# Attention with a gated MLP on one core: per-block output priority, a reciprocal as exp(-ln) on ScalarE, and a new order of the last four blocks

## The chip, the cores and the metric

The kernel runs on one core of a Trainium2 chip. A core has five engines that each work through a queue of their own in order: TensorE (PE, matrix products, with PEld for its weight loads), VectorE (DVE), ScalarE (ACT, activation functions), GpSimd (POOL) and SyncE (SP, which issues DMAs). Engines wait for each other through semaphores. The metric is device time in microseconds of one execution; lower is better.

## The reference

One token stream `x` of 2048 rows and 448 columns is normalised, and goes through attention with 16 heads of 28 columns and through a two-layer MLP; the product of the two branches is added to `x`:

```python
xn = _layernorm(x, axis=-1)
# A: attention
qkv = (xn @ wqkv).reshape(B, S, 3, H, Dh)      # H = 16, Dh = 28
scores = jnp.einsum("bhqd,bhkd->bhqk", q, k) * Dh ** -0.5
p = _softmax(scores, axis=-1)
o = jnp.einsum("bhqk,bhkd->bhqd", p, v)
s = o.reshape(B, S, D) @ wo
# B: MLP
h = _gelu(jnp.einsum("bsd,df->bsf", xn, w1) + b1)   # F = 1792
g = _silu(jnp.einsum("bsf,fd->bsd", h, w2) + b2)
return x + s * g
```

All arrays are bfloat16.

## The kernel before

**Blocks.** The attention is cut into 16 blocks (`NBLK`): four groups `g` of four heads, times four chunks `c` of 512 query rows. Block 4g+c has 64 steps `m`, each the scores of 128 keys against 512 queries for one head. Three more stages run beside the blocks: projections early, the MLP's first layer and GELU in the middle, its second layer (`p_f2`, 16 tiles), the gate (`p_silu`) and the output product with `wo` (`p_out`, `p_last`, 16 tiles of 128 rows) at the end. The output product of chunk c needs all four groups, so block 12+c (group 3) must be finished and normalised first.

**Softmax.** Scores of two or three steps go into banks of a PSUM ring (`t_score`), ScalarE takes exp of the two or three banks with one instruction (`p_exps`, 1024 or 1536 columns wide), and `t_pv` multiplies the result with the values and adds up in the bank `acc`. One column of the values gives the row sums. Some steps do not go through ScalarE: four steps at a time (a "quad") are sent to VectorE, which makes an approximate exp with integer arithmetic (`p_apass`, four instructions of 512 columns, then two more in `p_expq`); such steps are left out of ScalarE's list. `NQ` says how many quads each block tries for.

**Normalising a block.** `p_epi` copies `acc` to `E_sb` on VectorE, sends the four rows of sums by DMA to DRAM (`sums`) and back spread over 128 partitions (`rs`), takes the reciprocal on GpSimd (`rc`, a power of -1), sends it to DRAM (`recs`) and back broadcast (`x_sb<-recs`, four DMAs), and multiplies on GpSimd into `qT`. The last block is handled by quarters of 128 queries `t`: `p_epi4` copies a quarter out of `acc` (the last one on ScalarE, `EA = 1`), `p_norm4` spreads the sums over the partitions with one matmul against `selb`, takes a reciprocal on VectorE and multiplies; `p_last` then makes the output tile.

**Output tiles.** `t_oev` multiplies a finished `wo` product with the gate, adds `x` for chunks 2 and 3, and stores. A tile that comes after the last exp is copied from PSUM by ScalarE first, for those listed in `PATH`. The gate of the very last tile is made at the end (a tanh on ScalarE, two VectorE instructions).

**What sets the order.** A planner inside the kernel (`run`) lays down all five queues before anything executes. It keeps estimated durations for every task, and picks the next task of an engine by start time, then by a priority number (small goes first). Per block, `tune` overwrites a set of planner constants from the table `BP`: how early quads start, how many go with a group of scores, how many ring banks a group may take (`R3`), when the `t_pv` products are due, and so on. Which banks, fillers and quads fall where follows from these constants alone.

Of the kernel before, what the change touches and what calls it, by code (L numbers as in the profile page):

```python
# [16 lines left out]
DH = 28  # L17
F = 1792
G = 4
# [8 lines left out]
MTOT = NBLK * T * 4  # L28

GM = 584  # L30
BPN = ('MG', 'GQ', 'GE', 'EPS', 'PV0', 'PVC', 'MP', 'ND4', 'LU', 'JOINT', 'LQ', 'JMAX', 'DQ', 'URG', 'SLACK', 'UR', 'QLEAD', 'QDIST', 'R3')
BP = (
    (0, 7.789, 12, 0.114, 12, 2, 0.127, 4, 18, 0.15, 2, 2, 1, 7, 0.379, 1.063, -8, 20, 2),
    (0, 4.0, 12, 0.103, 12, 3, 0.124, 4, 16, 0.116, 2, 4, 8, 8, 0.359, 0.922, 18, 20, 0),
    (0, 4.0, 12, 0.1, 12, 3, 0.124, 4, 16, 0.02, 2, 3, 8, 9, 0.285, 0.922, 60, 31, 1),
    (1, 4.0, 11, 0.151, 12, 3, 0.124, 3, 14, 0.034, 2, 4, 10, 2, 0.413, 0.922, 58, 45, 1),
    (1, 4.0, 12, 0.1, 10, 4, 2.634, 4, 16, 0.232, 3, 5, 12, 17, 0.678, 0.922, -8, 20, 1),
    (1, 4.0, 12, 0.133, 18, 4, 0.124, 4, 17, 0.15, 2, 2, 8, 3, 0.413, 0.922, 60, 26, 1),
    (0, 4.0, 10, 0.143, 20, 1, 0.124, 6, 0, 0.15, 3, 5, 10, 4, 0.476, 2.281, 62, 36, 0),
    (0, 4.0, 22, 0.1, 29, 3, 0.034, 4, 15, 0.227, 6, 4, 6, 14, 0.306, 0.922, 60, 2, 3),  # L40
    (1, 4.0, 29, 0.182, 11, 1, 1.508, 2, 18, 0.237, 2, 4, 8, 8, 0.413, 0.922, 62, 12, 1),
    (1, 2.818, 8, 0.1, 6, 3, 0.124, 6, 5, 0.099, 5, 4, 8, 14, 0.378, 5.756, 60, 22, 1),
    (0, 4.0, 9, 0.079, 13, 3, 0.124, 5, 14, 0.094, 2, 2, 2, 22, 0.234, 0.623, 11, 12, 0),
    (0, 4.619, 12, 0.1, 12, 3, 0.124, 8, 2, 0.15, 2, 4, 6, 8, 0.244, 0.922, 60, 24, 0),
    (0, 5.612, 13, 0.1, 9, 2, 0.124, 4, 18, 0.375, 2, 4, 8, 9, 0.413, 0.922, -2, 16, 1),
    (1, 3.195, 12, 0.129, 17, 3, 0.124, 1, 0, 0.249, 2, 4, 10, 12, 0.413, 1.834, 60, 20, 1),
    (1, 4.0, 12, 0.109, 12, 3, 0.188, 4, 16, 0.131, 2, 4, 9, 22, 0.413, 0.922, 60, 20, 0),
    (0, 4.0, 12, 0.1, 12, 9, 0.124, 6, 18, 0.132, 2, 3, 8, 5, 0.342, 1.07, 56, 20, 2),
    (1, 4.0, 12, 0.1, 12, 3, 0.124, 4, 16, 0.15, 2, 4, 8, 10, 0.413, 0.922, 60, 20, 1),
)  # L50
NQ = (5, 11, 13, 13, 12, 7, 11, 10, 16, 3, 16, 16, 9, 14, 16, 16)
QLEAD, QDIST = 0, 12
JMAX, DQ, LQ, ND4, LU = 2, 3, 2, 3, 3
PV0, PVC, MP = 12, 4, 0.3
# [6 lines left out]
GP, MP4, GL = 4.64, 1, 1.2  # L61
URG = 12
SPR, AHEAD = 5, 101
R3 = 0
DUE, UR, M0, M2 = 13, 1.25, 59, 978
VT = (15, 14, 13, 12, 11, 10, 9, 8)
SM_SCALE = DH ** -0.5
# [21 lines left out]
EPS = 0.1  # L89
PVN = 2  # L90
OWN2 = 0
EA = 1
G3P = 0
PATH = {(1, 2): 'D', (1, 3): 'D', (2, 0): 'D', (2, 1): 'D', (2, 2): 'D', (2, 3): 'D'}
XADD = ()
OPR = (5, 5, 5)
OVERLAP = 0.083


# [26 lines left out]
class _Kernel:  # L126
# [258 lines left out]
    def alloc(self):  # L385
# [126 lines left out]
        self.b_selb = B()  # L512
        self.b_E4, self.b_on4, self.b_o4, self.b_o3 = ([B() for _ in range(4)] for _ in range(4))
        self.b_rf = [B(), B()]
        self.b_sum, self.b_sum2, self.b_m3 = B(), B(), B()
        self.b_sig3, self.b_g3 = B(), B()
        self.banks = [(self.misc[:, :], self.b_misc), (self.acc[:, :], self.b_acc)]
# [837 lines left out]
    def p_silu(self, c):  # L1355
        K = self
        yield ("until", lambda: K.f2n[c] == 4 and K.ready([K.b_fsb[c % 2]], 0.3) and (c < 2 or K.g_done[c - 2]))
        fb, sg = K.fsb[:, c % 2, :, :], K.sig[:, c % 2, :, :]
        nt = 4 if c < C - 1 else 3
        yield _Task(ACT, lambda eng: eng.activation(sg[:, 0:nt, :], fb[:, 0:nt, :], ACTF.Tanh, scale=0.5),  # L1360
                    [K.b_fsb[c % 2]], [K.b_sig[c % 2]], 0.1 + 0.375 * nt, 0.0, 0)
        if c < C - 1:
            for t in range(nt):
                o = K.g_sb[:, c, t, :]
                yield _Task(POOL, lambda eng, o=o, t=t: eng.tensor_tensor(o, sg[:, t, :], fb[:, t, :], ALU.mult),  # L1365
                            [K.b_sig[c % 2], K.b_fsb[c % 2]], [K.b_h[c], K.b_g[c]], 1.05, 0.05, 3, port=True)
                yield _Task(POOL, lambda eng, o=o, t=t: eng.tensor_tensor(o, o, fb[:, t, :], ALU.add),
                            [K.b_sig[c % 2], K.b_fsb[c % 2]], [K.b_h[c], K.b_g[c]], 1.05, 0.05, 3, port=True)
        for t0 in range(0, nt if c == C - 1 else 0, 2):
            t1 = min(t0 + 2, nt)  # L1370
            yield _Task(DVE, lambda eng, t0=t0, t1=t1: eng.scalar_tensor_tensor(
                K.g_sb[:, c, t0:t1, :], sg[:, t0:t1, :], 1.0, fb[:, t0:t1, :], op0=ALU.add, op1=ALU.mult),
                        [K.b_sig[c % 2], K.b_fsb[c % 2]], [K.b_h[c], K.b_g[c]], 0.15 + 0.467 * (t1 - t0), 0.0, 3)
        K.g_done[c] = True
        if c == C - 2:
            K.b_x2[c].r = list(K.b_h[c].r) + [K.b_h[c].w]
            for y in K.b_h[1], K.b_h[2]:
                K.b_x2[c].r += y.r + [y.w]
            xc = K.A_x[0].rearrange("(c p t) d -> c p t d", p=128, t=4)[c]
            for i in range(OWN2 // 2, 2):  # L1380
                dst = K.h[:, 1 + i, 5632:5632 + 2 * D].rearrange("p (t d) -> p t d", d=D)
                K.dma(SP, lambda eng, i=i, dst=dst: eng.dma_start(dst, xc[:, 2 * i:2 * i + 2, :]), K.s_x3, writes=[K.b_x2[c]] if i else [])
        if c < C - 1:
            return
        K.b_x2[c].r = list(K.b_h[c].r) + [K.b_h[c].w]
        K.dma(SP, lambda eng: eng.dma_start(K.x2[1][:, :, :], K.A_x[0].rearrange("(c p t) d -> c p t d", p=128, t=4)[c]),
              K.s_x2[c], writes=[K.b_x2[c]])
        if nt < 4:
            yield ("until", lambda: K.exp_m == MTOT - 1)
            o = K.g_sb[:, c, 3, :]  # L1390
            yield _Task(ACT, lambda eng: eng.activation(sg[:, 3, :], fb[:, 3, :], ACTF.Tanh, scale=0.5),
                        [K.b_fsb[c % 2]], [K.b_sig3], 0.47, 0.0, 0)
            E = POOL if G3P else DVE
            if not G3P:
                yield ("until", lambda: K.E_done == NBLK + 1)
            yield _Task(E, lambda eng: eng.tensor_tensor(o, sg[:, 3, :], fb[:, 3, :], ALU.mult),
                        [K.b_sig3, K.b_fsb[c % 2]], [K.b_h[c], K.b_g3], 1.05 if G3P else 0.39, 0.0, 2, port=E == POOL)
            if not G3P:
                yield ("until", lambda: K.on4[3])
            yield _Task(E, lambda eng: eng.tensor_tensor(o, o, fb[:, 3, :], ALU.add),  # L1400
                        [K.b_fsb[c % 2]], [K.b_h[c], K.b_g3], 1.05 if G3P else 0.39, 0.0, 2, port=E == POOL)

    def pieces(self, m):
        b, r = m // 64, m % 64
# [494 lines left out]
    def p_norm4(self, t):  # L1899
        K = self  # L1900
        g, c = G - 1, C - 1
        E, tE = K.E_sb[:, 1, 128 * t:128 * (t + 1)], K.b_E4[t]
        bank, tok = yield ("bank", lambda: K.g_done[C - 1] and K.ready([tE]), 3)
        yield _Task(PE, lambda eng: eng.matmul(bank[:, 0:128], K.selb[:, :], E, start=True, stop=True),
                    [tE, K.b_selb], [tok], 0.1, 0.12, 3)
        R = K.rf[:, t % 2, :]
        yield _Task(DVE, lambda eng: eng.reciprocal(R, bank[:, 0:128]), [tok], [K.b_rf[t % 2]], 0.96, 0.0, 1)
        K.banks.append((bank, tok))
        dst = K.qT[:, g, c * 512 + 128 * t:c * 512 + 128 * (t + 1)]
        yield _Task(DVE, lambda eng: eng.tensor_tensor(dst, E, R, ALU.mult), [tE, K.b_rf[t % 2], K.b_qT[g][c]],  # L1910
                    [K.b_on4[t]], 0.3, 0.0, 1)
        K.on4[t] = True

    def p_epi(self, b):
# [7 lines left out]
        yield ("until", lambda: K.late_on)  # L1922
        lag = 2.2 if b >= NBLK - 4 else 4.0
        src = bass.AP(tensor=K.E_sb, offset=DH * 1024 + 512 * (b % 2), ap=[[32 * 1024, 4], [1, 512]])
        K.dma(SP, lambda eng: eng.dma_start(K.sums.ap(), src), K.s_r[0], reads=[tE], writes=[K.b_sums],
              land=max(K.now, tE.tw) + lag)
        K.dma(SP, lambda eng: eng.dma_start(K.rs[:, :], K.sums.ap().rearrange("j (i k) -> (j i) k", k=16)), K.s_r[1],
              reads=[K.b_sums], writes=[K.b_srs], land=K.b_sums.tw + lag)
        yield _Task(POOL, lambda eng: eng.tensor_tensor(K.rc[:, :], K.rs[:, :], K.mone[:, 0:1].to_broadcast([128, 16]), ALU.pow),  # L1929
                    [K.b_srs, K.b_pads], [K.b_rc], 3.0, 0.05, 1)  # L1930
        K.dma(SP, lambda eng: eng.dma_start(K.recs.ap().rearrange("j (i k) -> (j i) k", k=16), K.rc[:, :]), K.s_r[2],
# [46 lines left out]
    
    def p_out(self, c, t):
        K = self  # L1980
        bank, tok = yield ("bank", lambda: K.pe_free() and K.on_done[(G - 1) * C + c] and K.g_done[c] and K.ready(K.b_onT[G - 1][c:c + 1]), OPR[c])
        K.pe_wait += 1
        ps = bank[:, 0:D]
        yield K.t_wo(ps, tok, c, t, (0, 1))
        yield K.t_wo(ps, tok, c, t, (2, 3))
        K.pe_wait -= 1
        yield from K.t_oev(ps, tok, c, t)
        K.banks.append((bank, tok))
# [63 lines left out]
```

## Time and profile before

| what | us |
|---|---|
| median of 3 runs (421.92 to 422.02) | 422.02 |
| the profiled execution's own time | 422.14 |
| its span, first to last instruction | 420.4 |
| TensorE busy | 401.6 |
| ScalarE busy | 406.6 |
| VectorE busy | 338.9 |
| GpSimd busy | 186.0 |
| granted TensorE clock, mean | 0.998 |
| window 302.47 to 341.60: ScalarE busy, VectorE busy | 38.75, 32.68 of 39.13 |
| window 341.60 to 391.60: ScalarE busy, VectorE busy | 49.98, 39.04 of 50.00 |
| window 391.60 to 410.34: ScalarE busy, VectorE busy | 18.74, 15.36 of 18.74 |
| window 410.34 to 420.40: ScalarE busy, TensorE busy | 3.02, 4.27 of 10.06 |

The four windows lie between the starts of the `acc` copies of blocks 10, 12 and 14, the end of the last exp, and the end of the span. Busy times are unions of an engine's instructions; activations overlap at their ends, so the sum of their durations is more than the time that they take, and the distance between two starts is the better measure. The engines' names and the source lines (L1480 is line 1480 of the kernel) are those of the profile.

### The profile page before, as it was taken

The numbers are of one execution on the slowest core, as the hardware profiler recorded it, in microseconds if no ns is written. First come the engines' busy times: TensorE is split into PE (matmuls) and PEld (weight loads), VectorE is DVE, ScalarE is ACT, GpSimd is POOL, SyncE is SP. The second block draws the span as 40 slices with busy tenths as digits, with TensorE's granted clock in tenths as the row PEclk, the third lists the DMA queues.
The fourth block names the chain that finished last, engine by engine and source line by source line (L and its number), as shares of the span: only waits on it lengthen the run. The fifth ranks groups of instructions, "written<-read, shape, count | busy, mean of one in ns | idle before, by whom it ended". The sixth has DMA issues, their size and how long they took to land.

```text
span 420.4 us, 9639 instructions
## 1 busy us (share of the span) xinstructions
PE 401.6 (96%) x3673; PEld 135.2 (32%) x3673; DVE 338.9 (81%) x588; ACT 406.6 (97%) x413; POOL 186.0 (44%) x193
## 2 busy tenths in 40 slices
PE   6999999999999999999999999999999999999994
PEld 4543223332222222223223433232222333223452
DVE  8968899997785899999893126799999675599885
ACT  6999999999999999999999999999999999999993
POOL 7571333237769271213331514408221947882420
PEclk9999999999999999999999999999999999999999
DMA  8701000000001001010320100000010001014142
GB/s 264 268 2 39 3 7 22 20 11 16 25 2 27 2 1 29 2 27 16 86 85 26 27 1 2 2 2 27 2 26 3 10 21 27 2 47 93 24 72 90
DMA packets 15912, 15.29 MB, mean 36 GB/s; under 512 B 7085, under 2 KB 12953, under 8 KB 15834
## 3 DMA queue, kind: packets, MB, share of 16 engines
q1 hardware_dynamic: 15002, 13.07, 11.1%
q0 software_dynamic: 576, 0.92, 1.7%
q8 instruction: 29, 0.48, 0.5%
q10 hardware_dynamic: 288, 0.69, 0.4%
q14 instruction: 17, 0.14, 0.1%
HBM read 12.60 MB, written 2.94 MB: 37 GB/s over the span
## 4 chain that ended last, share of the span: by engine, by line
PE 69%; ACT 15%; DVE 8%; issue 6%; POOL 1%; DVEq 0%; ACTq 0%; POOLq 0%
PE ring L1424 21%; PE acc L1860 16%; ACT P L1480 9%; PE ring L1275 9%; PE ring L1344 5%; PE ring L920 3%; ACT h L1480 3%; PE misc L920 3%; PE misc L1344 2%; ACT xnT L1480 2%; PE misc L1275 2%; PE misc L1214 2%; PE misc L1948 1%; PE ring L1214 1%; PE acc L1061 1%
## 5 line engine op out<-in xcount | busy, mean ns | idle before, releaser
L1480 ACT ACTIVATE P<-ring 128x1024 bf16<-128x1024 f32 (+1 forms) x238 | 253.5, 1179 | 1.4 <-PE ring L1424 0.6
L1424 PE MATMUL ring<-qT,kT 32*128 32x512 bf16 (+2 forms) x1049 | 141.9, 357 | 8.2 <-ACT P L1480 1.3
L1480 ACT ACTIVATE h<-ring 128x1024 bf16<-128x1024 f32 (+1 forms) x80 | 87.2, 1190 | 0.1
L1424 PEld LDWEIGHTS ring<-qT,kT 32*128 32x128 bf16 x1049 | 38.6, 91 | 143.4 <-ACT P L1480 82.9
L1929 POOL TENSOR_TENSOR rc<-rs,mone 128x16 f32<-128x16 bf16 x15 | 45.5, 3032 | 36.6 <-DMA rs<-sums 36.5
L1860 PE MATMUL acc<-P,vaug 128*32 128x512 bf16 (+2 forms) x621 | 53.9, 351 | 0.0
L1275 PE MATMUL ring<-xnT,w 128*128 128x512 bf16 x180 | 48.9, 382 | 0.0
L1480 ACT ACTIVATE xnT<-ring 128x1024 bf16<-128x1024 f32 (+1 forms) x37 | 43.1, 1203 | 0.1
L1938 POOL TENSOR_TENSOR qT<-x_sb,E_sb 128x512 bf16<-128x512 f32 x15 | 17.4, 1162 | 48.4 <-PE acc L1860 15.5
L1424 PE MATMUL misc<-qT,kT 32*128 32x512 bf16 (+1 forms) x103 | 38.4, 378 | 0.0
L1344 PE MATMUL ring<-w,h 128*128 128x448 bf16 x154 | 37.4, 355 | 0.4 <-DVE vaug L1709 0.3
L1709 DVE TENSOR_SCALAR x_sb<-ring 128x512 uint16<-128x512 f32 x40 | 27.1, 686 | 1.9 <-PE ring L1424 1.3
L1169 POOL TENSOR_TENSOR qsq<-qT 128x512 bf16<-128x512 bf16 x12 | 12.5, 1039 | 33.9 <-DVE qT L1163 31.4
L1860 PE MATMUL acc<-h,vaug 128*32 128x512 bf16 x222 | 27.1, 384 | 0.0
L1709 DVE TENSOR_SCALAR x_sb<-misc 128x512 uint16<-128x512 f32 x28 | 19.2, 686 | 4.8 <-PE misc L1424 4.0
L1275 PEld LDWEIGHTS ring<-xnT,w 128*128 128x128 bf16 x180 | 14.7, 97 | 23.8 <-issue 8.3
L1365 POOL TENSOR_TENSOR h<-w 128x448 bf16<-128x448 bf16 x12 | 12.7, 1055 | 21.8 <-DVE h L1768 14.5
L1709 DVE TENSOR_SCALAR h<-ring 128x512 uint16<-128x512 f32 x28 | 19.0, 686 | 0.3 <-PE ring L1424 0.2
L1860 PEld LDWEIGHTS acc<-P,vaug 128*32 128x32 bf16 x621 | 13.5, 95 | 16.3 <-issue 12.4
L1793 POOL TENSOR_SCALAR vs<-vaug 128x128 bf16<-128x128 bf16 x32 | 9.5, 297 | 20.6 <-DVE w L1768 18.0
L1259 DVE CAST h<-ring 128x512 bf16<-128x512 f32 x21 | 14.4, 686 | 4.4 <-PE ring L1275 4.3
L1344 PE MATMUL misc<-w,h 128*128 128x448 bf16 x70 | 17.1, 355 | 0.0
(266 smaller groups left out, 695.4 us busy)
## 6 DMA issues: line engine op xcount, KB each, us to landing
x_sb<-recs SPq DMA_DIRECT2D x60, 64.0 KB, 2.0
w<-in_B_w_dram SPq DMA_DIRECT2D x1, 1568.0 KB, 7.3
w<-in_B_w_dram SPq DMA_DIRECT2D x1, 1344.0 KB, 8.2
x_sb<-in_A_x_dram SPq DMA_DIRECT2D x2, 448.0 KB, 5.4
out_dram<-in_A_x_dram SPq DMA_DIRECT2D x2, 448.0 KB, 9.3
out_dram<-h POOLq DMA_DIRECT2D x4, 224.0 KB, 4.3
out_dram<-h SPq DMA_DIRECT2D x8, 112.0 KB, 1.7
h<-in_A_wqkv_dram SPq DMA_DIRECT2D x3, 168.0 KB, 5.1
```

The source lines that it names most:

```text
L920: return eng.matmul(bank, w[:, k, g * 128:(g + 1) * 128], K.xnT[:, k, c * 512:(c + 1) * 512], start=(k == 0), stop=(k == KT - 1))
L1214: ins = eng.matmul(bank[:, off:off + nh * DH], K.xnT[:, kt, t * 128:(t + 1) * 128], ap, start=(kt == 0), stop=(kt == KT - 1), skip_group_c ...
L1259: yield _Task(DVE, lambda eng: eng.tensor_copy(dst, bank), [tok], wr, 0.69, 0.0, 2)
L1275: return eng.matmul(bank, K.w1[:, k, ft * 128:(ft + 1) * 128], K.xnT[:, k, c * 512:(c + 1) * 512], start=(k == 0), stop=(k == KT - 1))
L1344: ins = eng.matmul(ps, hv[:, ft, t * 128:(t + 1) * 128], K.w2[:, ft, :], start=(ft == 0), stop=(ft == FT - 1))
L1365: yield _Task(POOL, lambda eng, o=o, t=t: eng.tensor_tensor(o, sg[:, t, :], fb[:, t, :], ALU.mult), [K.b_sig[c % 2], K.b_fsb[c % 2]], [K.b ...
L1424: return eng.matmul(dst, K.kT[32 * j:32 * j + 32, g, t * 128:(t + 1) * 128], K.qT[32 * j:32 * j + 32, g, c * 512 + q0:c * 512 + q0 + nq], ...
L1480: return eng.activation(reg[:, i0:i0 + n, :], K.ring[:, b0:b0 + n, :], ACTF.Exp, scale=SM_SCALE)
L1709: yield _Task(DVE, lambda eng: eng.tensor_scalar(K.part(u, k).bitcast(dt.uint16), K.like(u, bank), SM_SCALE * LOG2E * 128.0, (127.0 - EXP_ ...
L1860: return eng.matmul(K.acc[32 * j:32 * j + 32, q0:q0 + nq], w, ap[:, col:col + nq] if len(ap.shape) == 2 else ap[:, col // 128:(col + nq) / ...
L1929: yield _Task(POOL, lambda eng: eng.tensor_tensor(K.rc[:, :], K.rs[:, :], K.mone[:, 0:1].to_broadcast([128, 16]), ALU.pow), [K.b_srs, K.b_ ...
L1938: yield _Task(POOL, lambda eng: eng.tensor_tensor(dst, K.rb, E, ALU.mult), [K.b_rb, tE], [K.b_onT[g][c]], 1.15, 0.05, 1, port=True)
```

## The change

The diff has four parts.

1. A 20th column `OP` in the table: the priority of the output tiles of chunks 0 to 2, which was 5 for each, is 5 in blocks 0 to 12, then 4.26 in block 13, 5.041 in block 14 and 2.148 in block 15.
2. Rows 12 to 15 of the table have new numbers, and blocks 14 and 15 try for 14 quads where it was 16.
3. In the last block the last quarter's copy out of `acc` goes from ScalarE to VectorE (`EA = 0`); its reciprocal is made on ScalarE by ln and exp with a table load ahead of it (`LNR = 1`); and the spreading matmul may take a PSUM bank 0.35 us (planned) before its input is there.
4. Block 14's sums go straight from `E_sb` to `rs` in four small DMAs, where there was one to DRAM and one back.

```diff
-    (0, 5.612, 13, 0.1, 9, 2, 0.124, 4, 18, 0.375, 2, 4, 8, 9, 0.413, 0.922, -2, 16, 1),
-    (1, 3.195, 12, 0.129, 17, 3, 0.124, 1, 0, 0.249, 2, 4, 10, 12, 0.413, 1.834, 60, 20, 1),
-    (1, 4.0, 12, 0.109, 12, 3, 0.188, 4, 16, 0.131, 2, 4, 9, 22, 0.413, 0.922, 60, 20, 0),
-    (0, 4.0, 12, 0.1, 12, 9, 0.124, 6, 18, 0.132, 2, 3, 8, 5, 0.342, 1.07, 56, 20, 2),
+    (0, 5.612, 13, 0.1, 10, 4, 0.124, 4, 18, 0.375, 5, 4, 6, 9, 0.413, 0.922, 0, 12, 0, 5.0),
+    (1, 3.195, 12, 0.129, 6, 6, 0.124, 1, 0, 0.042, 1, 4, 10, 12, 0.413, 1.834, 77, 20, 1, 4.26),
+    (1, 5.574, 19, 0.109, 12, 5, 0.266, 3, 16, 0.061, 3, 3, 8, 4, 0.606, 0.922, 52, 39, 1, 5.041),
+    (0, 6.398, 12, 0.169, 12, 9, 0.124, 6, 18, 0.132, 2, 3, 8, 5, 0.342, 1.07, 56, 20, 2, 2.148),
...
-NQ = (5, 11, 13, 13, 12, 7, 11, 10, 16, 3, 16, 16, 9, 14, 16, 16)
+NQ = (5, 11, 13, 13, 12, 7, 11, 10, 16, 3, 16, 16, 9, 14, 14, 14)
...
-EA = 1
+EA = 0
+LNR = 1
...
+            if LNR:
+                K.prog[ACT].append(lambda eng: eng.preload_act_table_set("natural_log_exp_and_others"))
+                K.tE[ACT] += 1.3
...
-        bank, tok = yield ("bank", lambda: K.g_done[C - 1] and K.ready([tE]), 3)
+        bank, tok = yield ("bank", lambda: K.g_done[C - 1] and K.ready([tE], 0.35), 3)
...
-        yield _Task(DVE, lambda eng: eng.reciprocal(R, bank[:, 0:128]), [tok], [K.b_rf[t % 2]], 0.96, 0.0, 1)
+        if LNR and t == 3:
+            yield _Task(ACT, lambda eng: eng.activation(R, bank[:, 0:128], ACTF.Ln), [tok], [K.b_rf[t % 2]], 0.25, 0.0, 0)
+            yield _Task(ACT, lambda eng: eng.activation(R, R, ACTF.Exp, scale=-1.0), [K.b_rf[t % 2]], [K.b_rf[t % 2]], 0.25, 0.05, 0)
+        else:
+            yield _Task(DVE, lambda eng: eng.reciprocal(R, bank[:, 0:128]), [tok], [K.b_rf[t % 2]], 0.96, 0.0, 1)
...
+        if b == NBLK - 2:
+            for j in range(4):
+                one = bass.AP(tensor=K.E_sb, offset=(32 * j + DH) * 1024 + 512 * (b % 2), ap=[[1024, 1], [16, 32], [1, 16]])
+                K.dma(SP, lambda eng, j=j, one=one: eng.dma_start(K.rs[32 * j:32 * j + 32, :], one), K.s_r[1],
+                      reads=[tE], writes=[K.b_srs] if j == 3 else [], land=max(K.now, tE.tw) + lag)
...
-        bank, tok = yield ("bank", lambda: K.pe_free() and K.on_done[(G - 1) * C + c] and K.g_done[c] and K.ready(K.b_onT[G - 1][c:c + 1]), OPR[c])
+        bank, tok = yield ("bank", lambda: K.pe_free() and K.on_done[(G - 1) * C + c] and K.g_done[c] and K.ready(K.b_onT[G - 1][c:c + 1]), lambda: OP)
```

What this makes of the queues can be read from the built programs, without any time in them. All five queues are the same up to block 12. From there on:

| | before | changed |
|---|---|---|
| exps on ScalarE of 1024, 1536, 512 columns, from block 12's first group on | 51, 31, 1 | 55, 30, 0 |
| quads on VectorE, whole kernel | 59 | 58 |
| VectorE instructions between the `acc` copies of blocks 10 and 12 | 52 | 62 |
| output tiles behind the last exp on VectorE | 5, and the addition of a sixth | 3 |
| ScalarE copies of output tiles | 4 | 0 |
| exps between block 14's `acc` copy and chunk 2's first `wo` product | all that are left | about 9, each of 1536 |

Behind the last exp the changed queues hold, on TensorE: the last 32 `acc` products, one `wo` product, the spreading matmul, and two tiles of four `wo` products each; on ScalarE: the tanh of the last gate, the table load, ln, exp; on VectorE: the `acc` copy, a tile (multiply, add), half of the last gate, the last quarter's multiply, a tile, the other half of the gate, the last tile.

## The prediction

> **What bounds the kernel now.** I read the page first: busy shares and slices.
>
> ```profile
> PE 401.6 (96%) x3673; PEld 135.2 (32%) x3673; DVE 338.9 (81%) x588; ACT 406.6 (97%) x413; POOL 186.0 (44%) x193
> ACT   6999999999999999999999999999999999999993
> PE 69%; ACT 15%; DVE 8%; issue 6%; POOL 1%; DVEq 0%; ACTq 0%; POOLq 0%
> ```
>
> The third line is the chain of waits in the page's section 4; it names TensorE for most of the span, but a busy TensorE is not one that is late: ScalarE is full in every slice but the first and the last. So I took ScalarE's timeline (start, us, what; a row is a run of equal instructions).
>
> ```profile
> 302.09 7.46 ACT L1480 ACTIVATE P<-ring 128x1024 bf16<-128x1024 f32 x8
> 309.37 1.11 ACT L1480 ACTIVATE xnT<-ring 128x1024 bf16<-128x1024 f32 x1
> 389.83 2.87 ACT L1480 ACTIVATE xnT<-ring 128x1536 bf16<-128x1536 f32 x2
> 392.49 8.33 ACT L1480 ACTIVATE P<-ring 128x1536 bf16<-128x1536 f32 x7
> 405.04 5.40 ACT L1480 ACTIVATE P<-ring 128x1536 bf16<-128x1536 f32 x5
> 410.34 0.57 ACT L1391 ACTIVATE w<-w 128x448 bf16<-128x448 bf16 x1
> 411.28 0.28 ACT L1889 ACTIVATE E_sb<-acc 128x128 bf16<-128x128 f32 x1 [0.38 <-PE acc L1860]
> 412.13 0.54 ACT L1961 ACTIVATE h<-ring 128x448 bf16<-128x448 f32 x1 [0.57 <-PE ring L1948]
> ```
>
> Starts are what counts, since ends overlap. Eight exps of 1024 run from 302.09 to 309.37 with one short wait among them; the bare step is 0.904. Two of 1536 take 392.49 - 389.83 = 2.66, 1.33 each. The last exp is over at 410.34 (the tanh of L1391 follows at once), and 420.4 - 410.34 = 10.06 us of tail are left. The time is thus: ScalarE's work up to the last exp, plus its waits, plus the tail.
>
> **Part 1, ScalarE's work: +1.8.** The queues part at 315.77, where block 12's first exp starts. Before: 51 x 0.904 + 31 x 1.33 + 0.49 (the one of 512) + three tanhs (1.60, 1.60, 1.23, by their starts) = 92.25. Changed: 55 x 0.904 + 30 x 1.33 + 4.43 = 94.05. One quad less on VectorE is four steps more here. This is a count; I give it 0.1 either way. It is on the path.
>
> **Part 2, ScalarE's waits: -0.3.** Before, 410.34 - 315.77 = 94.57, so 94.57 - 92.25 = 2.32 us were waits, in pieces of 0.04 to 0.4. To see what the new order does to them I walked down two queues, TensorE's and ScalarE's, with distances between starts from TensorE's timeline: a score group 0.32 until other work starts, four `acc` products 0.215, two second-layer products 0.378, two `wo` products 0.38, 0.10 for going back to scores; a group starts 0.06 after the exp two before it ended and its exp at the earliest 0.45 later. For the queues before, this gives 1.4 of the 2.3, most of it where six or seven second-layer products stand between two groups (324.6 in the trace is one such place: `misc<-w,h` x10). In the new order fillers are spread more evenly and the walk gives 0.2. What the walk doesn't see (0.9 before: VectorE's banks, tanhs that wait for their input) I carry over at 0.8. From 0.5 to 1.5 for both together.
>
> A new wait comes on top. Chunk 2's first `wo` product now stands in TensorE's queue about nine exps of 1536, 9 x 1.33 = 12.0, behind the `acc` copy of block 14, with score groups queued behind it, and ScalarE waits for those. The chain that it needs, as it ran before:
>
> ```profile
> 391.60 0.69 DVE L1919 CAST E_sb<-acc 128x512 bf16<-128x512 f32 x1 [0.59 <-PE acc L1860]
> 392.32 0.49 SPq L1925 DMA_DIRECT2D sums<-E_sb  x1
> 393.93 0.34 SPq L1927 DMA_DIRECT2D rs<-sums  x1
> 395.59 3.44 POOL L1929 TENSOR_TENSOR rc<-rs,mone 128x16 f32<-128x16 bf16 x1 [5.65 <-DMA rs<-sums]
> 399.05 0.32 SPq L1931 DMA_DIRECT2D recs<-rc  x1
> 400.46 2.54 SPq L1934 DMA_DIRECT2D x_sb<-recs  x4
> 405.48 1.14 POOL L1938 TENSOR_TENSOR qT<-x_sb,E_sb 128x512 bf16<-128x512 f32 x1 [4.43 <-PE acc L1860]
> ```
>
> That is 15.02 us from copy to product. The direct DMAs take out one trip (393.93 - 392.32 = 1.61) but put four issues on SP in place of one: at steps of about 0.43 (the sixteen small `wo` loads at 33 us) the last leaves 1.3 after the first, and lands 1.6 after that (the row's median for `rs`), so `rc` starts 3.6 after the copy where it was 4.0: 0.4 gained, not 1.6. The rest varied over the 15 blocks: `rc` 2.9 to 3.44, the broadcast 3.3 to 4.9 from first issue to landing. So the chain takes 12.4 to 14.6. TensorE can wait until 12.4 after the copy before ScalarE runs dry (one exp of 0.904 and 0.45 of score time ahead, 0.96 for the four products in between). That is 0 to 2.3 us; block 14's broadcast was the slow one, beside GpSimd's output DMA, which stands in the same place now. I take 1.0. Waits in all: 0.2 + 0.8 + 1.0 = 2.0, against 2.32.
>
> **Part 3, the tail: -2.7.** Before, VectorE ended it:
>
> ```profile
> 411.11 0.39 DVE L1396 TENSOR_TENSOR h<-w 128x448 bf16<-128x448 bf16 x1
> 412.57 0.96 DVE L1907 RECIPROCAL w<-misc 128x128 f32<-128x128 f32 x1 [1.07 <-PE misc L1904]
> 416.53 0.69 DVE L1969 TENSOR_TENSOR h<-h 128x448 bf16<-128x448 bf16 x2
> L1327 ACT ACT_TABLE_LOAD x1 | 1.3, 1283 | 0.0
> ```
>
> The spreading matmul stood behind six `wo` products, the reciprocal idled 1.07 for it, and 12 instructions of chunks 2 and 3 followed until 417.21 (6.88 after the last exp); the last store was issued at 417.64. Changed, counted from the last exp: `acc` products done 0.89 (as before), copy 0.94 to 1.23, spreading matmul 1.46 to 1.68 behind one `wo` product. ScalarE: tanh to 0.57, table load 1.283 with 0.02 around it (it followed an exp 0.02 after its end at 252.46, and the next exp 0.01 after it), so ln starts at 1.87, after the matmul; ln and exp at about 0.3 each (the 128-column copy took 0.28) end at 2.5. VectorE meanwhile adds one tile and the gate's half (1.3 to 2.47), multiplies the quarter at 2.57, then tile (0.53 + 0.30), gate half 0.30, last tile 0.53 + 0.39: 4.85. Store at 4.9 against 7.30: 2.4 less. The last store landed 2.23 after issue, the others 1.7; with 0.3 for that, 2.7. From 2.0 to 3.1. The copy goes from ScalarE (0.28) to VectorE, idle then, at no cost. The table load is hidden by copy and matmul but for 1.87 - 1.73 = 0.14; without that cover it costs its 1.3.
>
> For the table switch, the Trainium skill (ScalarE: Activation LUTs, section "What ACT_TABLE_LOAD costs") states about 1283 ns for the load plus about 1380 ns of drain, 2.66 us for every switch. Ln would then start at 3.2 and the tail gain 1.3 instead of 2.7. The load's duration agrees to the nanosecond; the drain does not show in this trace, where load and its gaps take 1.31.
>
> Block priorities (`OP`) cost nothing by themselves: they moved chunk 2's four tiles ahead of the last exp, into TensorE's slack under the exps; without that cover they cost what the tail now saves.
>
> **Sum.** +1.8 - 0.3 - 2.7 = -1.2 on the profiled execution's 422.14 (420.4 of span, 1.7 around it), 420.9. The median of the runs is 0.1 lower: 420.8.
>
> **Rivals.**
> *No wait at chunk 2* (chain 12.4): waits 1.0, sum -2.2, 419.8. For it: the broadcast took 3.3 in most blocks. Against: not in block 14.
> *Full wait* (chain 14.6), or other waits as large as before: waits 3.3, sum +0.1, 422.1. For it: the planner's order fits a chain of 12, and GpSimd's DMAs stand beside it.
> *The table switch drains first*, for as long as the load itself takes (1.283, the row above): ln, exp and the five VectorE instructions behind them come 1.28 later, sum +0.1, 422.1. Against it: both loads inside the span followed their exp after 0.02. (The Trainium skill's section named above states such a drain.)
> *VectorE becomes the bound in blocks 11 and 12* (the other side). Between the copies of blocks 10 and 12 it now has 62 instructions for 40.3 us of ScalarE work, where it had 52 for 37.4 (32.68 busy of 39.13). For it, its rhythm in this stretch before:
>
> ```profile
> 317.99 0.69 DVE L1709 TENSOR_SCALAR wq<-misc 128x512 uint16<-128x512 f32 x1
> 318.60 0.68 DVE L1768 TENSOR_SCALAR vaug<-x_sb 128x2048 uint16<-128x2048 uint16 x1
> 319.26 0.69 DVE L1709 TENSOR_SCALAR wq<-misc 128x512 uint16<-128x512 f32 x1
> ```
>
> Two instructions take 319.26 - 317.99 = 1.27, so 62 need 39.4, just under 40.3. At 0.69 each, without overlap, they need 42.8 and ScalarE loses 2.5: sum +1.3, 423.3. It decides from 0.65 per instruction on; beside GpSimd's multiply at 405.48 one VectorE instruction (L1910) took 1.07 instead of 0.28, so stretching occurs. Against it: between 156 and 182 us VectorE was busy for 25.75 of 26, and ScalarE still for 25.99.
> *The change doesn't do what it says* has little room: the queues show each part.
>
> **How the numbers follow.** Forecast 0.45, no wait 0.15, full wait 0.18, drain 0.05, VectorE 0.17. About 0.2%, 0.84 us, is what a measurement of this kernel can tell from no change: faster is under 421.2, slower over 422.9. The first two are faster (0.60); full wait and drain are the same (0.23); VectorE is slower (0.17). The forecast's own range is 420.2 to 421.2 (chunk 2's wait between 0.4 and 1.4). The range goes from 419.4 (waits of 1.0 and a tail of -3.1) to 423.2 and so leaves out little more than half of the last case.
>
> **What would show it.** Last exp about 1.5 us later than 410.3 (411.8), tail of 7.4; TensorE idle before chunk 2's first `wo` product (L1962) with GpSimd's L1952 as releaser, about 1.0 in ScalarE's waits behind it; `rc` (L1943) of block 14 starting 3.6 after its copy; ln starting within 0.2 of the table load's end; ScalarE idle for VectorE's banks in block 12 under 0.8. A tail over 8.5, or waits over 3.5 in the last four blocks, would make it wrong.

## The result and the profile after

| | before | changed |
|---|---|---|
| median, us | 422.02 (5 runs, 421.9 to 422.13) | 427.41 (5 runs) |
| ratio, 95% interval | | 1.0126 [1.0112, 1.014] |
| span of the profiled execution | 420.4 | 425.5 |
| its granted clock, mean | 0.998 | 0.989 |

The changed kernel is 1.3% slower. Four of its runs lie between 426.44 and 428.72; one took 1173.25, which nothing here explains; the ratio leaves it out, and nothing below rests on it.

The page of the changed kernel first: busy shares, two of the slices, the chain of waits, and the group of exps (busy, mean ns of one, then idle time before it and who ended that).

```profile
PE 403.9 (95%) x3667; PEld 133.4 (31%) x3667; DVE 336.1 (79%) x582; ACT 407.8 (96%) x413; POOL 189.6 (45%) x197
ACT  6999999999999999999999999999999999999935
PEclk9999999999999999999999999999999999999968
PE 73%; ACT 12%; DVE 8%; issue 5%; DMA 1%; POOLq 0%; ACTq 0%; DVEq 0%
L1484 ACT ACTIVATE P<-ring 128x1024 bf16<-128x1024 f32 (+1 forms) x241 | 256.3, 1179 | 7.7 <-PE ring L1428 6.8
```

The fourth line is the chain of waits: it now has a share for DMA, 1% or some 4 us, which it had not before. ScalarE is full until the last two slices, where before only the last was thin; now the last but one is down to the digit 3 as well, and the clock falls to 0.6 there. The idle time that the exps spend on score groups, 6.8 us, is nearly all new: it was 0.6 before. ScalarE's timeline of the last 25 us shows where it lies (start, us, what; idle time before it and its releaser in brackets):

```profile
400.34 2.99 ACT L1484 ACTIVATE xnT<-ring 128x1536 bf16<-128x1536 f32 x2
403.00 1.25 ACT L1484 ACTIVATE P<-ring 128x1024 bf16<-128x1024 f32 x1
408.82 2.42 ACT L1484 ACTIVATE P<-ring 128x1536 bf16<-128x1536 f32 x2 [4.57 <-PE ring L1428]
413.12 5.05 ACT L1484 ACTIVATE P<-ring 128x1536 bf16<-128x1536 f32 x4 [1.88 <-PE ring L1428]
418.03 0.60 ACT L1392 ACTIVATE w<-w 128x448 bf16<-128x448 bf16 x1
418.64 1.28 ACT L1395 ACT_TABLE_LOAD   x1
419.94 0.28 ACT L1912 ACTIVATE w<-ring 128x128 f32<-128x128 f32 x1
```

Two waits, 4.57 and 1.88 as the trace counts them. Measured between starts, as the prediction did, they are 408.82 - 403.00 - 0.90 = 4.92, and 413.12 - 410.21 - 0.90 = 2.0 (the row at 408.82 names its first form only: its second exp, at 410.21, is one of 1024). The last exp ends at 418.03, not at 411.8; the tail behind it is 425.5 - 418.03 = 7.47.

So the 5.1 us of the spans divide into ScalarE's work +1.8, its waits from 2.32 to 8.29 (+5.97), and the tail from 10.06 to 7.47 (-2.6); the sum is +5.2, 0.1 over what the spans show.

What the waits hang on is block 14's way from `acc` to its multiply, and what lies around it:

```profile
389.86 0.68 DVE L1927 CAST E_sb<-acc 128x512 bf16<-128x512 f32 x1
390.56 2.50 SPq L1936 DMA_DIRECT2D rs<-E_sb  x4
392.02 0.87 POOL L1988 DMA_DIRECT2D out_dram<-h  x1 [3.12 <-DVE h L1979]
396.24 2.92 POOL L1943 TENSOR_TENSOR rc<-rs,mone 128x16 f32<-128x16 bf16 x1 [3.35 <-DMA rs<-E_sb]
399.13 0.90 POOL L1988 DMA_DIRECT2D out_dram<-h  x1
400.62 1.75 SPq L1948 DMA_DIRECT2D x_sb<-recs  x4
401.23 0.86 POOL L1988 DMA_DIRECT2D out_dram<-h  x1 [1.19 <-PE ring L1428]
406.10 1.15 POOL L1952 TENSOR_TENSOR qT<-x_sb,E_sb 128x512 bf16<-128x512 f32 x1 [4.02 <-DMA x_sb<-recs]
407.31 0.93 PE L1962 MATMUL ring<-wo,qT 128*128 128x448 bf16 x2 [4.16 <-POOL qT L1952]
408.17 0.61 PE L1428 MATMUL ring<-qT,kT 32*128 32x128 bf16 x12
```

The power (`rc`) starts 6.38 after the copy, where before's two trips gave 3.98, and the multiply 16.24 after it. TensorE stands for 4.16 before chunk 2's first product, with the score group for ScalarE behind it in its queue. The windows (length, busy time of PE, PEld, DVE, ACT and POOL, granted clock, share of the DMA engines, GB/s) show what follows:

```profile
403.00:408.80 5.80, 1.64 (x16) 0.58 (x16) 1.58 (x3) 1.25 (x2) 1.15 (x1) 0.78 0.38 69
408.80:412.00 3.20, 3.20 (x16) 1.11 (x16) 1.38 (x4) 2.42 (x2) 0.00 (x0) 0.50 0.11 36
412.00:418.00 6.00, 5.46 (x121) 2.88 (x120) 3.85 (x9) 4.88 (x4) 0.00 (x0) 0.91 0.18 60
```

Behind the pause the granted clock is 0.50. A score group takes 0.61 (the row at 408.17) instead of 0.40, and now TensorE is the late one: that is the second wait.

### The profile page after: what moved, and what is told of

Same layout as the page of the kernel before. It is cut to its first block, busy times and chain, and to the rows that moved or that the text cites. A ratio compares the mean times of both kernels' runs of the same rounds, so it can differ in the third digit from the quotient of the medians.

```text
span 425.5 us, 9623 instructions
## 1 busy us (share of the span) xinstructions
PE 403.9 (95%) x3667; PEld 133.4 (31%) x3667; DVE 336.1 (79%) x582; ACT 407.8 (96%) x413; POOL 189.6 (45%) x197
## 4 chain that ended last, share of the span: by engine, by line
PE 73%; ACT 12%; DVE 8%; issue 5%; DMA 1%; POOLq 0%; ACTq 0%; DVEq 0%
PE ring L1428 23%; PE acc L1864 16%; PE ring L1276 9%; PE ring L1345 7%; ACT P L1484 7%; PE ring L921 3%; PE misc L1345 3%; ACT h L1484 3%; PE misc L921 3%; PE misc L1276 2%; PE misc L1215 2%; ACT xnT L1484 1%; PE misc L1962 1%; PE ring L1215 1%; ACT h L1324 1%
## 5 line engine op out<-in xcount | busy, mean ns | idle before, releaser
L1484 ACT ACTIVATE P<-ring 128x1024 bf16<-128x1024 f32 (+1 forms) x241 | 256.3, 1179 | 7.7 <-PE ring L1428 6.8
L1943 POOL TENSOR_TENSOR rc<-rs,mone 128x16 f32<-128x16 bf16 x15 | 44.6, 2975 | 33.6 <-DMA rs<-sums 23.9
L1428 PE MATMUL misc<-qT,kT 32*128 32x512 bf16 (+1 forms) x97 | 36.9, 382 | 0.0
L1864 PE MATMUL acc<-h,vaug 128*32 128x512 bf16 (+1 forms) x230 | 27.6, 380 | 0.0
L1713 DVE TENSOR_SCALAR x_sb<-ring 128x512 uint16<-128x512 f32 x37 | 25.0, 686 | 2.1 <-PE ring L1428 1.8
L1713 DVE TENSOR_SCALAR h<-ring 128x512 uint16<-128x512 f32 x32 | 21.8, 686 | 0.4 <-PE ring L1428 0.2
```

Of the source, the lines that this page charges most:

```text
L1428: return eng.matmul(dst, K.kT[32 * j:32 * j + 32, g, t * 128:(t + 1) * 128], K.qT[32 * j:32 * j + 32, g, c * 512 + q0:c * 512 + q0 + nq], ...
L1484: return eng.activation(reg[:, i0:i0 + n, :], K.ring[:, b0:b0 + n, :], ACTF.Exp, scale=SM_SCALE)
L1713: yield _Task(DVE, lambda eng: eng.tensor_scalar(K.part(u, k).bitcast(dt.uint16), K.like(u, bank), SM_SCALE * LOG2E * 128.0, (127.0 - EXP_ ...
L1864: return eng.matmul(K.acc[32 * j:32 * j + 32, q0:q0 + nq], w, ap[:, col:col + nq] if len(ap.shape) == 2 else ap[:, col // 128:(col + nq) / ...
```

## The experiments

Three theories stood at the start. **A**: GpSimd's accumulating output transfers of chunks 0 and 1 (`out_dram<-h` on POOL) hold up block 14's small transfers. **B**: the four direct transfers are slow by themselves. **C**: the halved clock behind the pause is a loss of its own.

**no_out_dma.** The four output transfers are left out, so the output of chunks 0 and 1 stays at `x`.

```diff
-        elif t % 2:
+        elif t % 2 and False:
```

> The changed kernel without GpSimd's four accumulating output DMAs of chunks 0 and 1 (that part of the output stays x alone); all queues otherwise as they were. Theory A (the output DMAs, which now run beside block 14's normalisation, hold up its small DMAs): the direct DMAs land within 4.2 us of the copy (6.31 before), rc starts by 4.3 after it, the broadcast lands 3.3 to 3.6 after its first issue (5.4 before), the product is there 13 after the copy, TensorE stands less than 0.5 us before chunk 2's first output product (4.2 before), and the last exp ends near 411.5 (418.0 before). Rival B (four 32-byte-piece DMAs between partitions are slow by themselves): rc still starts 6 or more after the copy, and TensorE still stands 2 us or more.

Measured in a single run: 420.82, span 419.0, clock 0.998. The sums landed 4.37 after the copy (6.31 in the changed kernel; within 4.2 was expected), the broadcast took 3.38 from first issue to landing (5.41), the multiply started at +12.24, and ScalarE's wait was 0.22. A is right that the chain is slow only beside these transfers. But this leaves work out, so it is not yet a kernel.

**warm_wait.** 72 matmuls of 128 columns ahead of chunk 2's first product keep TensorE at work in the pause.

```diff
+        if (c, t) == (2, 0):
+            def f(eng):
+                ins = None
+                for _ in range(72):
+                    ins = eng.matmul(bank[:, 0:128], K.zero[:, :], K.ident[:, :], start=True, stop=True)
+                return ins
+            K.put(_Task(PE, f, [K.b_id, K.b_pads], [tok], 0.0, 0.0, 0))
```

> The changed kernel with 72 matmuls of 128 columns by zeros put ahead of chunk 2's first output product, which fill about 3.8 of the 4.2 us for which TensorE stands there; nothing else moves. Theory C (the halved clock after the idle stretch costs time of its own, the 2.0 us wait behind it above all): the granted clock stays at 1.0 until the last exp, the second wait falls from 2.0 to under 0.3, the first stays at 4.5 to 4.9, time 424.8 to 425.5. Rival D (the second wait comes from the order, with or without the clock): time stays within 0.5 of 427.4.

Measured: 425.19, ratio 1.0076 [1.0058, 1.0094], clock 0.999. The first wait stays (4.21, a little under the expected 4.5), the second is gone. C is right, and its share is 1.0126 - 1.0076, about 2 us.

**two_trips.** Part 4 undone: row sums as before, all else changed.

```diff
-        if b == NBLK - 2:
-            for j in range(4):
...
+        K.dma(SP, lambda eng: eng.dma_start(K.sums.ap(), src), K.s_r[0], reads=[tE], writes=[K.b_sums],
+              land=max(K.now, tE.tw) + lag)
+        K.dma(SP, lambda eng: eng.dma_start(K.rs[:, :], K.sums.ap().rearrange("j (i k) -> (j i) k", k=16)), K.s_r[1],
+              reads=[K.b_sums], writes=[K.b_srs], land=K.b_sums.tw + lag)
```

> The changed kernel with block 14's sums again by DRAM (part 4 undone); the planner then counts one trip more and puts chunk 2's first output product one exp later, with a tile of chunk 3 ahead of it. Theory A: rc starts 4 to 5 after the copy, the chain takes 15 to 16, TensorE stands 0 to 1.5 us, the clock stays up until the last exp, time 420.5 to 422.0. Rival E (the new order of the last block waits in any case): two waits of over 4 us together remain, time 425 or more.

Measured: 422.25, ratio 1.0006 [0.9996, 1.0017], 0.25 over the expected range. The power starts at +3.91, the multiply at +12.32, the wait is 0.18. The rival, that the new order waits in any case, falls, and the whole loss goes with part 4. But the planner, which reckons with the longer way, also lays the end out otherwise: chunk 2's last tile comes after chunk 3's, and the tail is 8.40. Transfers and order are still mixed.

**direct_alone.** Before plus the four direct transfers, the planner told the old landing time, so that the order stays before's.

```diff
+        if b == NBLK - 2:
+            for j in range(4):
+                one = bass.AP(tensor=K.E_sb, offset=(32 * j + DH) * 1024 + 512 * (b % 2), ap=[[1024, 1], [16, 32], [1, 16]])
+                K.dma(SP, lambda eng, j=j, one=one: eng.dma_start(K.rs[32 * j:32 * j + 32, :], one), K.s_r[1],
+                      reads=[tE], writes=[K.b_srs] if j == 3 else [], land=max(K.now, tE.tw) + 2 * lag)
```

> The kernel before with part 4 alone: block 14's sums by four direct DMAs, the planner still counting two trips, so that only SyncE's queue differs. There the output DMA of chunk 0 is issued 2.7 us ahead of block 14's copy. Theory A: the direct DMAs land within 4.5 us of the copy, rc starts by 4.5. Rival B: rc starts 6 or more after the copy. In both the time stays within 0.5 of 422.0, since chunk 2's products stand behind the last exp there.

Measured in a single run: 421.24, 0.26 under the expected 421.5 to 422.5, beside 421.79 for before, not enough to tell them apart. The power starts at +4.41: B falls, four direct transfers undisturbed take 4.4. That is still 0.5 more than two trips (3.9), not less. The broadcast took 5.4 here, beside an output transfer issued 0.35 ahead of it.

**defer_out.** The changed kernel with nothing left out; the output transfers that are ready before block 14's multiply are issued right behind it. All other queues keep their order.

```diff
+            if K.on_done[NBLK - 2]:
+                put()
+            else:
+                K.held.append(put)
...
         K.on_done[b] = True
+        if b == NBLK - 2:
+            for put in K.held:
+                put()
```

> The changed kernel whole, but GpSimd issues the four accumulating output transfers of chunks 0 and 1 only after block 14's last multiply; every other instruction on every engine stays in its order and nothing is left out. A (these transfers hold block 14's row sums and reciprocals up): the sums land by +4.4 after the copy instead of +6.3, the broadcast takes 3.4 instead of 5.4, the multiply starts by +12.4 instead of +16.2, the wait at chunk 2's first output product is under 0.4, the granted clock stays at 0.99, last exp at 411.6, time 420.5 to 421.3 (faster than before by 0.2 to 0.35%). B (the four direct transfers are slow by themselves): sums at +6 or later, 425 or more. E (taking the transfers away helped only because they were gone, and put later they hold up the output transfers of the last chunks instead): the wait is gone, but the tail grows past 8.5 and the time is 422 or more.

Measured: 420.99, ratio 0.9984 [0.9973, 0.9995]; sums at +4.36, broadcast 3.27, multiply at +12.13, wait 0.21, last exp at 411.58, tail 7.4. A, with each of its numbers. E falls: chunk 2's stores on SP now land up to 6.2 after their issue, but chunk 3's, which come last, land after 1.7 to 2.4, and the tail doesn't grow.

**part3_alone** and **rows_alone** take the change apart at the other end. The first has before's tables and way of the sums with part 3 only; the second parts 1 and 2 only.

```diff
 part3_alone, against before
-EA = 1
+EA = 0
+LNR = 1
...
-        bank, tok = yield ("bank", lambda: K.g_done[C - 1] and K.ready([tE]), 3)
+        bank, tok = yield ("bank", lambda: K.g_done[C - 1] and K.ready([tE], 0.35), 3)
...
 rows_alone, against the changed kernel
-EA = 0
-LNR = 1
+EA = 1
+LNR = 0
...
-        bank, tok = yield ("bank", lambda: K.g_done[C - 1] and K.ready([tE], 0.35), 3)
+        bank, tok = yield ("bank", lambda: K.g_done[C - 1] and K.ready([tE]), 3)
...
```

> Before's two tables and row sums by two trips, with only the edits at the end of the kernel (last reciprocal as ln and exp on ScalarE, the spreading product's bank 0.35 sooner, EA 0). My record gave the tail -2.7. If that stands without the new tables: last exp 410.2 as before, tail 7.4 to 7.9 instead of 10.1, time 419.3 to 420.2. Rival: with before's order all four output tiles of chunk 2 stand behind the last exp too, and they, not the reciprocal, set the end: tail 9 to 10, time 421 to 422.

> The new table rows, output priorities and counts alone (parts 1 and 2): row sums of block 14 by two trips, the end of the kernel as before (EA 1, reciprocal on VectorE). If the parts add up: ScalarE's work +1.8 and last exp at 411.9 as in the kernel with two trips, tail 10.1 as before, time 423.5 to 424.0. Rival: the new order also shortens the tail, because chunk 2's output tiles leave it: tail 8 to 9, time 421.7 to 422.7, and then part 3 was given too much of the tail's gain.

Measured: 422.14, ratio 1.0001 [0.9991, 1.0012], and 422.13, ratio 1.0013 [1.0003, 1.0022]. Both rivals hold, part3_alone's slightly outside its numbers. Part 3 without the new order gains nothing; VectorE's timeline of part3_alone says why:

```profile
412.61 0.29 DVE L1918 TENSOR_TENSOR qT<-E_sb,w 128x128 bf16<-128x128 bf16 x1 [0.79 <-ACT w L1913]
414.50 0.69 DVE L1977 TENSOR_TENSOR h<-h 128x448 bf16<-128x448 bf16 x2
416.57 0.38 DVE L1971 TENSOR_TENSOR h<-h 128x448 bf16<-128x448 bf16 x1
416.98 0.39 DVE L1977 TENSOR_TENSOR h<-h 128x448 bf16<-128x448 bf16 x1
```

The last quarter is multiplied at 412.61, in good time, and then the tiles of chunk 2 that stand behind the last exp follow until 417.4. The tail is 10.45, a little over the rival's 9 to 10. The rows alone give a tail of 8.43.

**honest_late.** The changed kernel, the planner told that block 14's broadcast lands 5 us later.

```diff
-        K.mark(h, [K.b_recs], [K.b_rb], K.b_recs.tw + lag + 0.6)
+        K.mark(h, [K.b_recs], [K.b_rb], K.b_recs.tw + lag + 0.6 + (5.0 if b == NBLK - 2 else 0.0))
```

> The changed kernel, with the planner told that block 14's broadcast lands 5 us later than it assumed (about what the trace shows); transfers as in the changed kernel. If the loss comes from the order made on a wrong time of this chain: chunk 2's output products move behind the last but one exp, the wait of 4.9 and the slow clock after it go (ScalarE idle under 1.5 from 403 to the last exp, clock 0.99), last exp at 411.5 to 412, tail 8 to 9.5 because chunk 2's tiles now stand in it; time 420.5 to 422.5. Rival (the score products, not the order of the output products, wait behind the chain in some other way): over 424.

Measured: 422.99, ratio 1.0037 [1.0023, 1.0051]. The waits are gone and the last exp ends at 410.72, 0.8 sooner than expected, although the multiply starts only at +16.1; but chunk 2's tiles are back in the tail, 10.43, more than the 8 to 9.5 expected, and the time is above my range. An order that knows the slow chain avoids the wait and loses the gain.

**order_alone.** The order of the changed kernel on PE, ACT and DVE (the planner reckons with the direct landing time), but the sums go by two trips; the output transfers stay where they are in GpSimd's queue.

```diff
-        if b == NBLK - 2:
-            for j in range(4):
...
+        K.dma(SP, lambda eng: eng.dma_start(K.rs[:, :], K.sums.ap().rearrange("j (i k) -> (j i) k", k=16)), K.s_r[1],
+              reads=[K.b_sums], writes=[K.b_srs], land=max(K.now, tE.tw) + lag if b == NBLK - 2 else K.b_sums.tw + lag)
```

> The changed kernel with block 14's row sums by two trips in fact, while the planner goes on reckoning with the landing time of the direct transfers: so the order of TensorE, ScalarE and VectorE is the changed kernel's, and the output transfers are where the changed kernel has them in GpSimd's queue. F (the order is harmless, the direct transfers start the loss: their last lands among the output transfer, which makes the power late, and the next output transfer queued behind the power then meets the broadcast): sums at +3.9, power from +4.0, output transfers issued at +6.8 and +11.4, broadcast landed by +11.8, multiply at +12.3, wait at chunk 2's first product under 0.5, time 420.8 to 421.4. G (the new order alone costs the wait, with any way of the sums): wait of 2 or more, time 423 or more.

Measured: 421.22, ratio 0.9983 [0.9969, 0.9996], the gain back by the sums' way alone. Its timeline, to be read against the changed kernel's above:

```profile
390.06 0.68 DVE L1927 CAST E_sb<-acc 128x512 bf16<-128x512 f32 x1
390.77 0.49 SPq L1933 DMA_DIRECT2D sums<-E_sb  x1
392.22 0.87 POOL L1982 DMA_DIRECT2D out_dram<-h  x1 [3.12 <-DVE h L1973]
392.38 0.33 SPq L1935 DMA_DIRECT2D rs<-sums  x1
393.98 2.92 POOL L1937 TENSOR_TENSOR rc<-rs,mone 128x16 f32<-128x16 bf16 x1 [0.89 <-DMA rs<-sums]
396.86 0.90 POOL L1982 DMA_DIRECT2D out_dram<-h  x1
398.34 1.73 SPq L1942 DMA_DIRECT2D x_sb<-recs  x4
402.38 1.15 POOL L1946 TENSOR_TENSOR qT<-x_sb,E_sb 128x512 bf16<-128x512 f32 x1
```

The output transfer is issued 2.16 after the copy in both kernels. Here the power starts at +3.92. The next output transfer, queued behind the power on GpSimd, leaves at +6.80 and not at +9.27, lands by +10.8, and the broadcast by +12.2 (+11.8 was expected). F holds: the order is harmless, and the direct transfers start the loss.

The transfers' own records in the traces, in us after the copy, show how narrow this is (first start to last end, records, longest record):

```
                        sums' last piece        output transfer
order_alone     rs      3.26 - 3.52  x144       3.61 - 5.84  x144, 1.10
defer_out       rs      3.88 - 4.04  x48        (none yet)
changed         rs      5.08 - 5.81  x48        3.60 - 5.79  x144, 1.12
                        broadcast               output transfers
order_alone     x_sb    9.67 - 11.76 x192       8.27 - 10.43, then from 12.78
changed         x_sb   12.23 - 15.82 x192      10.74 - 16.02 x288, 1.11
```

The second trip is through 0.09 before the output transfer's first record. The fourth direct piece, due at 3.88, comes into it and ends with it; the three pieces before had escaped. The Trainium skill (DMA: Bandwidth & Descriptors, section "Queues, rings and completion order") states that a DMA engine goes round the queues that have work for it and takes a whole packet of one before it turns to the next. The trace agrees: the output transfer has 128 data records and 16 completion records, and in the changed kernel each of the fourth piece's 16 completion records ends 0.015 behind one of those 16 (5.11 to 5.81 behind 5.10 to 5.80). The records do not name their engine, but by these times the piece came through on each engine only when that engine's share of the output transfer, eight data records and a completion, was done. The broadcast, too, starts with the first completion record of the output transfer ahead of it (both at 12.23). Whether this share is one packet the records do not say.

**defer_c1_only.** As defer_out, but chunk 0's pair stays in its old place.

```diff
-            if K.on_done[NBLK - 2]:
+            if c == 0 or K.on_done[NBLK - 2]:
```

> The changed kernel, with only chunk 1's two output transfers put after block 14's multiply; chunk 0's stay. If each pair holds up its own step: sums still at +6.2 to +6.4 (chunk 0's second transfer lies beside them), broadcast 3.4 instead of 5.4 long, multiply at +14.1 to +14.3, wait at chunk 2's first product 2.0 to 2.4, time 422.8 to 424.5 by whether the clock drops behind so short a wait. Rival: the hold of the sums comes from chunk 1 in some way: sums by +4.4, time 421.

Measured: 425.53, ratio 1.0084 [1.0059, 1.0109]. The sums land at +6.24, so that hold is chunk 0's; the broadcast takes 3.95 and not 3.4, with no output transfer beside it (what took the 0.6 stays open), and the multiply starts at +14.71. ScalarE waits 2.47 and then 1.30. The first wait is just over the expected 2.4; the time is over my range, since the clock falls here too. TensorE's timeline:

```profile
405.97 0.55 PE L1966 MATMUL ring<-wo,qT 128*128 128x448 bf16 x2 [2.64 <-POOL qT L1953]
406.46 0.40 PE L1429 MATMUL ring<-qT,kT 32*128 32x128 bf16 x12
408.28 1.70 PE L1966 MATMUL ring<-wo,qT 128*128 128x448 bf16 x4
409.91 0.61 PE L1429 MATMUL ring<-qT,kT 32*128 32x128 bf16 x12
```

It comes back at full speed (0.55, 0.40) and is slow only 1.7 us later (0.61).

**defer_no3.** defer_out with part 3 undone, by the same edit as in rows_alone.

```diff
-EA = 0
-LNR = 1
+EA = 1
+LNR = 0
...
```

> The changed kernel with the output transfers of chunks 0 and 1 after block 14's multiply, and with part 3 undone (reciprocal on VectorE, copy of the last E on ScalarE, spreading product's bank as before). Last exp at 411.6 to 411.8 in either case. My record's step (part 3 is worth the whole 2.7 of the tail): tail 10.0, time 423.6. Rival (the order of chunk 2's tiles already gives some 1.6 of it, as the kernel with parts 1 and 2 alone showed, and part 3 only the rest): tail 8.3 to 8.6, time 422.0 to 422.4.

Measured: 421.84, ratio 0.9998 [0.9984, 1.0011], tail 8.30. VectorE's timeline, first of defer_no3, then of defer_out:

```profile
413.30 0.96 DVE L1916 RECIPROCAL w<-ring 128x128 f32<-128x128 f32 x1 [0.19 <-PE ring L1909]
414.36 0.29 DVE L1919 TENSOR_TENSOR qT<-E_sb,w 128x128 bf16<-128x128 bf16 x1
416.98 0.39 DVE L1987 TENSOR_TENSOR h<-h 128x448 bf16<-128x448 bf16 x1
```

```profile
414.14 0.29 DVE L1919 TENSOR_TENSOR qT<-E_sb,w 128x128 bf16<-128x128 bf16 x1
416.46 0.39 DVE L1987 TENSOR_TENSOR h<-h 128x448 bf16<-128x448 bf16 x1
```

The last exp ended at 411.24 and 411.58, so the last addition starts 5.74 and 4.88 after it: with the order given, part 3 is worth 0.86. The rival's tail holds; the time is 0.2 under its range, and in the profiled execution the last exp ended 0.4 sooner than expected.

**defer_order.** order_alone with the output transfers behind the multiply: both edits together.

```diff
+            if K.on_done[NBLK - 2]:
+                put()
+            else:
+                K.held.append(put)
...
+              reads=[K.b_sums], writes=[K.b_srs], land=max(K.now, tE.tw) + lag if b == NBLK - 2 else K.b_sums.tw + lag)
```

> The order of the changed kernel, row sums by two trips in fact, and the output transfers of chunks 0 and 1 after the multiply: no direct transfers and no collision. Sums at +3.9, multiply at +11.5 to +11.8, wait at chunk 2's first product under 0.3, last exp 411.7, tail 7.3, time 420.7 to 421.2, the same as with the direct transfers. If it is faster than that by 0.5 or more, the direct transfers cost something beyond the chain.

Measured: 420.79, ratio 0.9976 [0.9963, 0.9989], multiply at +11.56, no wait at chunk 2's product. It beats both kernels; its interval overlaps those of defer_out and order_alone, so the three are not told apart.

| | ratio to before | multiply after copy | ScalarE's idle times from chunk 2's product on | tail |
|---|---|---|---|---|
| changed | 1.0126 | 16.24 | 4.57 + 1.88 | 7.4 |
| warm_wait | 1.0076 | 16.44 | 4.21 | 7.4 |
| defer_c1_only | 1.0084 | 14.71 | 2.47 + 1.30 | 7.4 |
| honest_late | 1.0037 | 16.10 | none | 10.4 |
| rows_alone | 1.0013 | 12.32 | 0.17 | 8.4 |
| two_trips | 1.0006 | 12.32 | 0.18 | 8.4 |
| part3_alone | 1.0001 | 13.87 | none | 10.4 |
| defer_no3 | 0.9998 | 12.15 | 0.22 | 8.3 |
| defer_out | 0.9984 | 12.13 | 0.21 | 7.4 |
| order_alone | 0.9983 | 12.32 | 0.22 | 7.4 |
| defer_order | 0.9976 | 11.56 | none | 7.5 |

## Why the prediction was wrong

**The step that failed** is the chain of block 14 in part 2, "12.4 to 14.6", and with it the wait of 1.0 at chunk 2's first product. Copy to product took 407.31 - 389.86 = 17.45, and the wait with what came behind it 4.92 + 2.0. Undisturbed, the chain takes 13.35 (defer_out), inside the recorded bounds; what broke them is the second of these three points, which the first made possible:

- The direct transfers. The record has "steps of about 0.43", the last landing 1.6 later and the power at +3.6. The steps were 0.64 and undisturbed the power starts at +4.4 (direct_alone, defer_out). Part 4 makes the chain 0.5 longer instead of 0.4 shorter. A step taken from loads of another shape was too short.
- "GpSimd's output DMA, which stands in the same place now". In the queue, yes; in time, no. Against the copy, chunk 0's second transfer moved from -2.68 to +2.16, and chunk 1's from +8.53 and +14.97 to +9.27 and +11.37. So one fell on the sums and two on the broadcast, and the power's delay itself pushed the first of these two there (+6.80 in order_alone). That overlap is the term that the chain left out: 17.45 - 13.35 = 4.1 us. The upper bound of 14.6 came from rows with other neighbours, so it was no bound.
- The clock behind the pause, about 2 us, was in no term.

**What held.** ScalarE's work, +1.8: work and waits (94.05 and 8.29) make up the 102.3 us from block 12's first exp to the last to within 0.1. The small waits in the four blocks were 1.37 where the record had 1.0, none over 0.23, so VectorE did not become the bound. The table switch took 0.02 + 1.28 + 0.01 before ln; no drain shows. The tail, 7.4 by the record, was 7.47.

**Right in size, not divided.** The record has the tail's 2.7 as one sum over the changed queues. It says of the new order only that chunk 2's tiles, without the cover of the exps, would cost "what the tail now saves", and the first expectation for part3_alone gave the whole 2.7 to part 3 of the change. The runs divide it: 1.6 are the order's (rows_alone), 0.9 part 3's, and these only when chunk 2's tiles are out of the way (defer_no3); part 3 alone has 0.

**The rivals.** "Full wait" had the mechanism and named the transfers beside it, with a wait of 2.3 instead of 6.9. Slower was given only to VectorE, wrongly. The table switch that drains and VectorE as the bound did not occur.

So the gain was there, and was lost in one place. At full clock ScalarE loses nothing when chunk 2's first product starts by 13.1 after the copy: with the waits measured between starts, 15.91 cost 2.82 (defer_c1_only), 13.53 cost 0.43 (order_alone) and 13.35 cost 0.23 (defer_out). The record's 12.4 was 0.7 too strict, and the changed kernel's product starts at 17.45. With that mended in three ways the time is 420.8 to 421.2.

## What to carry to other kernels

An order that takes work into slack under a long chain turns every microsecond of that chain beyond the slack into time of the bound: measure the chain where it will stand, with the transfers that will then run beside it, and don't take its bounds from where it stood. Fewer hops were not a shorter way here, where one hop became four issues on a queue (power at +4.4 against +3.9); and a bulk transfer that nobody waits for belongs behind the small ones on which an engine waits. Part a gain by undoing its pieces singly: two edits that only work together look like one.

## What the runs showed of the hardware

A granted clock of 0.5 came after a pause of less than 3.41 us, and late. By the traces' clock records it lasted, after the pause of 4.16, from 406.27 to 413.10, 6.83 us; in defer_c1_only, after one of 2.64, from 407.69 to 411.10, 3.41 us, beginning 1.7 after TensorE was at work again. The lengths are two and one times 3.41. The Trainium skill (TensorE: Matmul & The Clock Gate, section "What's actually happening") states free-running windows of 3413 ns and a fall after at least one idle window. The lengths agree, and in both traces the fall lies 399.36 us, 117 times 3.413, behind the clock's first rise; the condition doesn't: a pause of 2.64 cannot fill a window of 3.41, and in the 3.41 us ahead of defer_c1_only's fall TensorE stood for 405.97 - 404.28 = 1.69 and worked for the rest. The measurement decides; what share of a window is enough, these runs don't show.

The last of four transfers of 1 KB in pieces of 32 bytes landed 1.9 us later (6.31 against 4.36 after the copy), and a broadcast of 256 KB went from 3.3 to 5.4, while one or two accumulating transfers of 224 KB were under way; the DMA engines as a whole were far from full in the first case (share 0.56 in the 3.7 us around it).
